# Moving two small expert groups ahead of the token groups of the second and third batch (Trainium2, one core)

## The chip, the cores and the metric

The kernel runs on one core of a Trainium2 chip. The metric is the device time of one execution in microseconds (us). Engines are named as in the profile: PE is TensorE (matrix products), PEld its weight loads, DVE is VectorE, ACT is ScalarE, POOL is GpSimd, SP is SyncE. SP and POOL issue nearly all DMA transfers; each issues in program order, so a transfer that has to wait holds up everything behind it on the same engine ("SPq" is SP as a DMA queue).

## The reference

Two blocks follow each other. The first is an attention over 4 batches of 1088 tokens with 4 heads of 32 columns, whose result is the input x (4352 tokens by 128 columns) of the second, a mixture of 8 experts. All experts see all tokens; P is a table of weights made by 8 rounds of normalizing rows and columns.

```python
# attention: phi(x) = outer product of S1 x and S2 x, 64 features
kv = einsum('bhsf,bhsd->bhfd', phi(k), v);  z = sum(phi(k), axis=2)
x  = einsum('bhsf,bhfd->bhsd', phi(q), kv) / (einsum('bhsf,bhf->bhs', phi(q), z) + 1e-06)
# experts: N, D, E, F = 4352, 128, 8, 1024
P = exp(x @ w_gate - max)
for _ in range(8):
    P /= P.sum(1, keepdims=True) + 1e-09; P /= P.sum(0, keepdims=True) + 1e-09; P *= N / E
out = sum(P[:, e:e+1] * (relu(x @ w1[e]) @ w2[e]) for e in range(E))
```

## The kernel before, in words

**Two phases of expert work.** The program keeps PE busy with expert products while attention and the routing (the 8 rounds that make P) are still running. In this first phase, which ends at 209 us, it works through a list `groups`. A large group `(lo, n, [0])` is expert 0 on 2n tokens from token lo; it needs those columns of xT, the transposed x. A small group `(0, REST, [e])` is expert e on the first 256 tokens only, which are the tokens 0 to 255 of the first batch. Routing weights are put on afterwards, so the groups do not have to wait for P. In the second phase (L1084, L1134) experts 1 to 7 run on all other tokens, with weights first recombined by DVE and POOL ("forms"); that phase takes the remaining 700 us and is not touched.

**Steps.** `steps()` (L886 to L920) is a generator. One step does the first product of one block of the hidden layer (L787, two matmuls of n columns, each as two passes on the chip, so that the profile counts four), a relu on ACT (L789), and the second products of a block that was begun eight steps earlier (`LAG`, L851). A large group has 16 steps, a small one 8, and the whole list 152. Every step is worth a share of `n / 480` (times 16/15 where the seven-product form isn't used). The attention and routing generators yield how many shares of expert work to run between two of their own pieces; `fill` runs steps until that is paid. So the order of PE's instructions is fixed when the program is built, and PE executes it in order.

**Where x comes from.** Batch 0 is made in place on the core (`divide`). Batches 1 to 3 go another way: `tops` (L486) gives numerator and denominator on PE, `over` (L499 to L505, DVE) divides and transposes, and `take_over` writes the result to memory (xd<-xt, L510) and reads it back into xT (xT<-xd, four transfers, L512). For batches 1 and 2 POOL issues both; for batch 3 POOL issues two thirds and SP the rest. A large group that starts at token 1088 needs batch 1, the one at 1920 batches 1 and 2, and so on.

**Where weights come from.** `wb` has six parts of 1024 columns: parts 0 to 2 hold expert 0, parts 3 and 4 first expert 1 (`load_w`) and later another small expert (`small_load`). `prepare_w` issues the loads of expert 1. `bench_load` and `bench_pack` prepare packed weights of experts 4 and 5 for the second phase during attention(2): bench_load(0) brings raw weights into xf0, bench_pack(0) forms their sums on POOL (L201, xf<-xf) and stores them (packed<-xf, L247), and bench_load(2) brings the next raw weights into the same xf0, so SP holds it back until that store has finished. In the routing stage `small_weights` loads experts 3, 5, 6, 7 and one more expert in xf0.

**End of the first phase.** `t0` is the number of steps ahead of the small groups at the list's end. From there on, the program places `first_forms` (DVE, L986 to L990), the weighting of the second item and the forms of five weight halves (`forming`, DVE L1046) among the remaining steps.

Of the kernel before, what the change touches and what calls it, by code (L numbers as in the profile page):

```python
# [53 lines left out]
def kernel(  # L54
# [18 lines left out]
    F = moe_w1.shape[2]  # L73
# [18 lines left out]
    wb = big.tile([P, 6 * F], F32, name="wb")  # L92
# [100 lines left out]
    def load_w(e):  # L193
        w1, w2, ws = (wb[:, F * (3 * e + i):F * (3 * e + i + 1)] for i in range(3))
        w2, ws = w2.rearrange("p (f d) -> p f d", d=DM), ws.rearrange("p (c q d) -> p c q d", c=4, d=H2)
        nc.sync.dma_start(out=w1, in_=moe_w1[e])
        nc.sync.dma_start(out=w2, in_=moe_w2[e].rearrange("(fo fi) d -> fi fo d", fi=P))
        return [w1, w2, None, ws]
# [14 lines left out]
    def sums_of_two(w2, ws):  # L213

        forms(w2[:, 0::2, 0:H2], w2[:, 1::2, 0:H2], w2[:, 0::2, H2:DM], w2[:, 1::2, H2:DM], *(ws[:, i] for i in range(4)),
              False)
        return ws
# [105 lines left out]
    def transpose_k(b, parts=((0, NT),)):  # L323
        kx = loaded["k", b]
        for lo, hi in parts:
            nc.vector.transpose(out=kT[:, 0:NT * P].rearrange("p (t c s) -> p c t s", c=4, s=32)[:, :, lo:hi],
                                in_=kx[:, 0:4 * NT, :].rearrange("p (c t) d -> p c t d", c=4)[:, :, lo:hi])
        nc.vector.transpose(out=kT[:, NT * P:S], in_=kx[:, 4 * NT:SA, :].rearrange("p a d -> p (a d)"))
# [77 lines left out]
    def multiply(c, i):  # L406
        lo, hi = chunks[c]
        nc.vector.tensor_tensor(phs[0][:, i, lo:hi], phs[0][:, i, lo:hi], queries.pop((0, c, i)), op=Alu.mult)
# [192 lines left out]
    def routing():  # L601
# [53 lines left out]
        for b in range(B):  # L655
# [13 lines left out]

    NX = 256  # L670
    REST = 256
    groups = [(0, 256, [0]), (512, 288, [0]), (1088, 416, [0]), (0, REST, [1]), (1920, 416, [0]), (2752, 416, [0]),
              (0, REST, [2]), (3584, 384, [0]), *((0, REST, [e]) for e in (4, 3, 5, 6, 7))]
    SMALL = {g for g, group in enumerate(groups) if group[2][0]}
    DIRECT = {0, *SMALL}
    HELD = 2
# [2 lines left out]
    items = [(g, e) for g, group in enumerate(groups) for e in group[2]]  # L679
# [3 lines left out]
    def direct_of(j):  # L683
        return items[j][0] in DIRECT

    def prepare_w(j):
        e = items[j][1]
        if e not in loaded_w and e < 2:
            loaded_w[e] = load_w(e) if j else first_w
# [101 lines left out]
    def two(k):  # L791

        j, q = blocks[k]
        lo, n, _ = groups[items[j][0]]
        h, ts, (later_h, earlier_h, t13) = hs[k] = room_of(k)

        def step(c):
            f, t = (4 * q + c, 0) if items[j][0] in SMALL else (2 * q + c // 2, c % 2)
            first(k, f, lo + t * n, lo + (t + 1) * n, h[c], k % 2)

        def less(out, a, b):
            nc.vector.tensor_tensor(out, a, b, op=Alu.subtract)

        def sums(c):
            if direct_of(j):
                return
            if c == 4:
                less(t13, later_h, earlier_h)
            elif c == 5:
                less(ts[2], h[3], ts[0])  # L810
                less(ts[3], h[2], ts[2])

        return step, sums
# [63 lines left out]
    def second(k, p):  # L877
        into(items[blocks[k][0]][0], *p)

    def steps():  # L880

        todo, sums_at, t = {}, {}, 0
        for k in range(len(blocks)):
            if k < len(blocks):
                j, q = blocks[k]
                g, e = items[j]  # L886
                n = groups[g][1]
                if q == 0:
                    for i in (j, j + 1):
                        if i < len(items):  # L890
                            prepare_w(i)
                if j == 6 and q == 0:
                    small_load(4, wb[:, 3 * F:4 * F], wb[:, 4 * F:5 * F])
                if q == 1 and j + 1 < len(items) and not direct_of(j + 1):
                    w = loaded_w[items[j + 1][1]]
                    if w[2] is None:
                        w[2] = sums_of_two(w[1], w[3])
                step, sums_ = two(k)
                products = eight if g in DIRECT else seven
            for c in range(4):  # L900
                if k < len(blocks):
                    step(c)
                for do in sums_at.pop(t, ()):
                    do()
                while soon:
                    soon.pop(0)()
                for b, p in todo.pop(t, ()):
                    second(b, p)
                if k < len(blocks) and c == 0:
                    for i in range(2, 10):  # L910
                        sums_at.setdefault(t + i, []).append(lambda i=i, f=sums_: f(i))
                    for i, ps in enumerate(products(k)):
                        if j < len(items) - HELD:
                            todo.setdefault(t + LAG + i, []).extend((k, p) for p in ps)
                        else:
                            held.append((loaded_w[e][1][:, 4 * q + i], hs[k][0][i]))
                share = n / 480 * (16 / 15 if g in DIRECT else 1)
                if later and (c % 2 or share > 0.9 or k >= len(blocks)):
                    later.pop(0)()
                yield share  # L920
                t += 1
# [70 lines left out]
    def small_weights():  # L992

        spare = [pools[0].tile([P, 7, 2, NX], F32, tag="ht", name="ht").rearrange("p s a n -> p (s a n)") for _ in range(2)]
        xf0 = xfs[0].rearrange("p f n -> p (f n)")
        places = {3: (spare[0], 0, 1), 5: (spare[1], 0, 1), 2: (xf0, 0, 1)}
        for e, (t, i, k) in places.items():
            small_load(e, t[:, F * i:F * (i + 1)], t[:, F * k:F * (k + 1)])
        small_load(6, spare[0][:, 2 * F:3 * F], wb[:, 5 * F:6 * F])
        small_load(7, spare[1][:, 2 * F:3 * F], None)  # L1000

    def small_load(e, w1, w2):
        if w1 is not None:
            loaded_w[e] = [w1, None, None, None]
            tc.keep_in_program_order(nc.sync.dma_start(out=w1, in_=moe_w1[e]))
        if w2 is not None:
            w2 = loaded_w[e][1] = w2.rearrange("p (f d) -> p f d", d=DM)
            tc.keep_in_program_order(nc.sync.dma_start(out=w2, in_=moe_w2[e].rearrange("(fo fi) d -> fi fo d", fi=P)))
# [341 lines left out]
    with tc.manual_schedule(engines={engines.DVE, engines.PE}):  # L1350
        for i in range(2):
            multiply(1, i)
        transpose_k(1)
        load_k(2)
        fill(1.25)
        fractions(1, 1)
        fractions(1, 0)
        fill(0.75)
        divide(1)
        keys_ab(1)  # L1360
        fill(0.75)
        query_products(2)
        keys_products(1, 0)
        fill(0.75)
        for i in range(2):
            multiply(2, i)
        keys_products(1, 1)
        fill(1.5)
        fractions(2, 1)
        fractions(2, 0)  # L1370
        keys_products(1, 2)
        fill(0.75)
        divide(2)
        load_v(2)
        load_q(3)
        fill(0.5)
        for b in range(1, B):
            for n in attention(b):
                fill(n)
        for n in routing():  # L1380
            fill(n)
        weights_first()
        t0 = sum(4 * (2 if g in SMALL else 4) for g in range(8))
        assert ran[0] > t0 - 8
        turn_first()
        forming = [lambda e=e, half=half, n=n: form_step(e - 1, half, n) for e, half in AHEAD for n in range(4)]
        for n, (e, half) in enumerate(AHEAD):
            forming.insert(5 * n + 4, lambda e=e, half=half: keep_formed(e - 1, half))
        among = {t0 + 10: [first_forms],
                 t0 + 12: [lambda do=do: do(1) for do in (weights, weighted, turn, xsums)],  # L1390
                 t0 + 18: [lambda: small_load(7, None, wb[:, 4 * F:5 * F])]}
        while ran[0] < 4 * len(blocks):
            for do in among.pop(ran[0], ()):
                do()
            if ran[0] > t0 + 3 and forming:
                forming.pop(0)()
            next(work)
            ran[0] += 1
        assert not soon and not later and not forming and not among
# [40 lines left out]
```

## Time and profile before

| | |
|---|---|
| median of 3 runs | 912.89 us (912.67 to 914.03) |
| the profiled execution's own time | 911.29 us |
| its span, first to last instruction | 909.2 us (2.1 us lie around it) |
| its mean granted TensorE clock | 0.994 |
| PE busy | 892.0 us, 98% of the span |
| DVE, ACT, POOL busy | 734.4, 526.1, 365.5 us |
| HBM read, written | 148.38 MB, 18.65 MB |

The profile page splits the span into 40 slices of 22.7 us and shows each engine's busy share in tenths. Other views are cut from the same execution: the waits (who waited for whom), the chain of work that ended last, the timelines of single engines, and the windows (busy time of each engine in chosen stretches, with the granted clock). Times in the views are in us from the span's start.

### The profile page before, as it was taken

The numbers are of one execution on the slowest core, as the hardware profiler recorded it, in microseconds if no ns is written. First come the engines' busy times: TensorE is split into PE (matmuls) and PEld (weight loads), VectorE is DVE, ScalarE is ACT, GpSimd is POOL, SyncE is SP. The second block draws the span as 40 slices with busy tenths as digits, with TensorE's granted clock in tenths as the row PEclk, the third lists the DMA queues.
The fourth block names the chain that finished last, engine by engine and source line by source line (L and its number), as shares of the span: only waits on it lengthen the run. The fifth ranks groups of instructions, "written<-read, shape, count | busy, mean of one in ns | idle before, by whom it ended". The sixth has DMA issues, their size and how long they took to land.

```text
span 909.2 us, 34647 instructions
## 1 busy us (share of the span) xinstructions
PE 892.0 (98%) x14664; PEld 710.9 (78%) x14664; DVE 734.4 (81%) x1160; ACT 526.1 (58%) x1276; POOL 365.5 (40%) x381
## 2 busy tenths in 40 slices
PE   8969999999999999999999999999999999999997
PEld 6747756688898877787777888999789886788776
DVE  7647778873899888889889897988889788889984
ACT  3325546466655665666566656665755676567652
POOL 3010330040454444545674453435434553544330
PEclk9979999999999999999999999999999999999999
DMA  9896359061577867778787777777676777767740
GB/s 263 261 314 192 118 177 303 1 216 71 169 222 231 240 197 215 219 235 231 214 237 197 222 213 226 214 218 226 200 200 196 234 217 221 227 201 220 198 125 13
DMA packets 150234, 183.97 MB, mean 202 GB/s; under 512 B 16352, under 2 KB 112368, under 8 KB 149696
## 3 DMA queue, kind: packets, MB, share of 16 engines
q1 hardware_dynamic: 143856, 164.17, 61.4%
q0 software_dynamic: 5024, 17.42, 5.4%
q8 instruction: 116, 1.90, 0.8%
q14 instruction: 38, 0.31, 0.1%
q10 hardware_dynamic: 1200, 0.16, 0.1%
HBM read 148.38 MB, written 18.65 MB: 184 GB/s over the span
## 4 chain that ended last, share of the span: by engine, by line
PE 95%; DMA 2%; DVE 1%; issue 0%; SPq 0%; ACT 0%; POOL 0%; ACTq 0%
PE a L1084 37%; PE s L1134 37%; PE a L787 9%; PE s L851 7%; PE a L371 1%; DMA xd<-xt 1%; PE s L866 1%; DMA xT<-xd 1%; PE a L486 1%; DMA qx<-in_q_dram 1%; PE a L1235 0%; PE s L400 0%; PE s L416 0%; PE a L450 0%; PE a L520 0%
## 5 line engine op out<-in xcount | busy, mean ns | idle before, releaser
L1084 PE MATMUL a<-wb,w1f 64*64 64x256 f32 x4144 | 430.0, 377 | 0.0
L1084 PEld LDWEIGHTS a<-wb,w1f 64*64 64x64 f32 x4144 | 269.9, 133 | 37.2 <-issue 2.2
L1084 PE MATMUL a<-xf,w1f 64*64 64x256 f32 x2128 | 229.2, 377 | 0.4 <-issue 0.4
L1098 ACT COPY a<-a 128x256 f32<-128x256 f32 x224 | 80.0, 357 | 212.1 <-PE a L1084 211.9
L1134 PE MATMUL s<-ht,w2r 64*64 64x256 f32 x1344 | 189.2, 376 | 0.0
L1134 PE MATMUL s<-hb,w2r 64*64 64x256 f32 x1344 | 187.5, 376 | 0.0
L201 POOL TENSOR_TENSOR wb<-wb 128x256 f32<-128x256 f32 (+1 forms) x115 | 130.4, 1135 | 125.4 <-DMA wb<-wb 78.6
L1134 PE MATMUL s<-ht,w2f 64*64 64x256 f32 x1216 | 160.3, 376 | 0.0
L1134 PE MATMUL s<-hb,w2f 64*64 64x256 f32 x1216 | 158.4, 376 | 0.0
L1084 PEld LDWEIGHTS a<-xf,w1f 64*64 64x64 f32 x2128 | 139.9, 133 | 19.0 <-issue 1.5
L1134 PEld LDWEIGHTS s<-ht,w2r 64*64 64x64 f32 x1344 | 113.1, 133 | 19.9
L1134 PEld LDWEIGHTS s<-hb,w2r 64*64 64x64 f32 x1344 | 112.3, 133 | 18.3
L789 ACT ACTIVATE hb<-a 128x256 f32<-128x256 f32 (+3 forms) x152 | 66.2, 441 | 82.6 <-PE a L787 74.1
L787 PE MATMUL a<-xT,wb 128*64 128x416 f32 (+3 forms) x448 | 102.6, 462 | 7.6 <-DMA xT<-xd 7.6
L1134 PEld LDWEIGHTS s<-ht,w2f 64*64 64x64 f32 x1216 | 99.0, 133 | 9.1
L1134 PEld LDWEIGHTS s<-hb,w2f 64*64 64x64 f32 x1216 | 98.3, 133 | 8.2
L851 PE MATMUL s<-hb,wb 128*64 128x416 f32 (+3 forms) x408 | 98.9, 455 | 0.0
L201 POOL TENSOR_TENSOR xf<-xf 128x256 f32<-128x256 f32 (+1 forms) x62 | 71.1, 1149 | 61.9 <-DMA xf<-xf 43.2
L1105 DVE TENSOR_TENSOR ht<-a,mid 128x256 f32<-128x256 f32 x112 | 47.2, 422 | 58.6 <-ACT a L1093 40.6
L201 POOL TENSOR_TENSOR wb<-wb,xT 128x512 f32<-128x512 f32 x37 | 51.4, 1388 | 88.3 <-DMA wb<-pT 65.0
L1093 ACT COPY a<-a 128x256 f32<-128x256 f32 x224 | 80.0, 357 | 9.3 <-PE a L1084 1.0
L1096 ACT COPY mid<-a 128x256 f32<-128x256 f32 x224 | 85.0, 379 | 0.0
(203 smaller groups left out, 1636.7 us busy)
## 6 DMA issues: line engine op xcount, KB each, us to landing
w1f<-packed SPq DMA_DIRECT2D x204, 224.0 KB, 5.0
w2r<-in_moe_w_dram SPq DMA_DIRECT2D x56, 512.0 KB, 7.1
w2f<-packed SPq DMA_DIRECT2D x68, 256.0 KB, 4.9
wb<-pT SPq DMA_DIRECT2D x45, 256.0 KB, 4.6
wb<-wb SPq DMA_DIRECT2D x74, 128.0 KB, 4.4
hb<-packed SPq DMA_DIRECT2D x32, 256.0 KB, 6.3
xf<-pT SPq DMA_DIRECT2D x19, 256.0 KB, 4.4
xf<-xf SPq DMA_DIRECT2D x36, 128.0 KB, 4.1
```

The lines of the kernel that those rows point to most:

```text
L201: tc.keep_in_program_order(nc.gpsimd.tensor_tensor(*args, op=op))
L371: nc.tensor.matmul(pv[64 * s:64 * (s + 1), i], kp[0:n, H * t + h].rearrange("p i j -> p (i j)"), vx[0:n, slots[h], t, :], start=(t == 0 an ...
L486: nc.tensor.matmul(pn[64 * s:64 * (s + 1), t, 2 * i:2 * i + 2].rearrange("p h d -> p (h d)"), ph[:, i, s, 64 * t:64 * (t + 1)], kvs[b % 2] ...
L787: nc.tensor.matmul(ph[sl], loaded_w[items[j][1]][0][:, P * f + H2 * s:P * f + H2 * (s + 1)], xT[:, lo:hi], start=True, stop=True, tile_pos ...
L789: nc.scalar.activation(out=out, in_=ph, func=Act.Relu)
L851: nc.tensor.matmul(sums[g][i][H2 * s:H2 * (s + 1)], w, x, start=c == 1, stop=c == per, tile_position=(0, H2 * s))
L1084: nc.tensor.matmul(half_of(r, b, c, n)[rows[s]], w1s[i][rows[r], 1 + form, u, H2 * s:H2 * (s + 1)], xf(i, x)[rows[r]], start=m == opens, s ...
L1093: nc.scalar.copy(b, a)
L1096: nc.scalar.copy(m5s[k, r], c)
L1098: nc.scalar.copy(d, a)
L1105: nc.vector.tensor_tensor(h[:, H3, r], d, m5s[k, r], op=Alu.add)
L1134: nc.tensor.matmul(place[rows[s]], w[form][rows[r], pair, u], h[rows[r], x, pair], start=task in (0, 4) and k in firsts, stop=True, tile_p ...
```

## The change

The list of groups gets another order. In words, with large groups by their first token: before, 0, 512, 1088, e1, 1920, 2752, e2, 3584, then e4, e3, e5, e6, e7; after, 0, 512, e1, 1088, e2, 1920, 2752, e4, 3584, then e3, e5, e6, e7. What goes with it: the load of expert 1 is issued at the third block of the first group instead of when the group ahead of it starts; parts 3 and 4 of wb take expert 2 after expert 1 (`small_load(2)`, placed at the third block of group 1088) instead of expert 4; expert 4 takes the place in xf0 that expert 2 had; the second weights of expert 7 are loaded when the group e4 starts instead of near the end of the phase; and t0 counts nine groups instead of eight, since five small groups at the end have become four.

```diff
-    groups = [(0, 256, [0]), (512, 288, [0]), (1088, 416, [0]), (0, REST, [1]), (1920, 416, [0]), (2752, 416, [0]),
-              (0, REST, [2]), (3584, 384, [0]), *((0, REST, [e]) for e in (4, 3, 5, 6, 7))]
+    groups = [(0, 256, [0]), (512, 288, [0]), (0, REST, [1]), (1088, 416, [0]), (0, REST, [2]), (1920, 416, [0]),
+              (2752, 416, [0]), (0, REST, [4]), (3584, 384, [0]), *((0, REST, [e]) for e in (3, 5, 6, 7))]
...
                 if q == 0:
-                    for i in (j, j + 1):
-                        if i < len(items):
-                            prepare_w(i)
-                if j == 6 and q == 0:
-                    small_load(4, wb[:, 3 * F:4 * F], wb[:, 4 * F:5 * F])
+                    prepare_w(j)
+                if j == 0 and q == 2:
+                    prepare_w(2)
+                if j == 3 and q == 2:
+                    small_load(2, wb[:, 3 * F:4 * F], wb[:, 4 * F:5 * F])
+                if j == 7 and q == 0:
+                    small_load(7, None, wb[:, 4 * F:5 * F])
...
-        places = {3: (spare[0], 0, 1), 5: (spare[1], 0, 1), 2: (xf0, 0, 1)}
+        places = {3: (spare[0], 0, 1), 5: (spare[1], 0, 1), 4: (xf0, 0, 1)}
...
-        t0 = sum(4 * (2 if g in SMALL else 4) for g in range(8))
+        t0 = sum(4 * (2 if g in SMALL else 4) for g in range(9))
...
-                 t0 + 12: [lambda do=do: do(1) for do in (weights, weighted, turn, xsums)],
-                 t0 + 18: [lambda: small_load(7, None, wb[:, 4 * F:5 * F])]}
+                 t0 + 12: [lambda do=do: do(1) for do in (weights, weighted, turn, xsums)]}
```

## The prediction

> **What bounds the kernel now.** First the page: PE is busy for 892.0 of 909.2 us, so only what makes PE wait or run slowly can be won. Its slices show where that is.
>
> ```profile
> PE   8969999999999999999999999999999999999997
> PEclk9979999999999999999999999999999999999999
> ```
>
> The only dip behind the start is in the third slice (45 to 68 us), and the granted clock dips there too. The waits and the chain of work say for what:
>
> ```profile
> PE a L787 <- DMA xT<-xd: 7.6, 1, 7.6
> ```
>
> ```profile
> 46.69 8.46 DMA xd<-xt
> ...
> 57.07 6.22 DMA xT<-xd
> ```
>
> This is the first product of group 1088, which needs batch 1 in xT; x goes out to memory and back, 14.7 us in two transfers. PE's timeline and the windows (wall time, busy time of five engines, granted clock, DMA share, GB/s) give the price:
>
> ```profile
> 55.50 0.41 PE L851 MATMUL s<-hb,wb 128*64 128x288 f32 x1
> 63.53 1.65 PE L787 MATMUL a<-xT,wb 128*64 128x416 f32 x4 [7.63 <-DMA xT<-xd]
> ...
> 65.90 3.90 PE L371 MATMUL a<-v,kp 128*64 128x64 f32 x72
> 69.74 0.92 PE L787 MATMUL a<-xT,wb 128*64 128x416 f32 x4
> ```
>
> ```profile
> 56.00:58.00 2.00, 0.00 (x0) 0.00 (x0) 1.32 (x2) 0.79 (x3) 2.00 (x4) 1.00 1.13 240
> 58.00:60.00 2.00, 0.00 (x0) 0.00 (x0) 1.97 (x4) 0.00 (x0) 1.22 (x3) 0.73 1.09 244
> ...
> 66.00:68.00 2.00, 2.00 (x42) 2.00 (x40) 0.00 (x0) 0.00 (x0) 0.00 (x0) 0.50 0.95 332
> ```
>
> PE stops at 55.9. The clock falls to half at about 58.9 and stays there until about 69.1, so the work from 63.53 to 69.74 (6.2 us) is what takes 3.6 us elsewhere: 0.70 for a first product of 416 columns, 0.48 for second products of 288, 2.39 for keys_sums (L371, at 92.95). **Price of the wait: 7.6 + 2.6 = 10.2 us**, 1.1% of the run.
>
> **The change part by part.** No matmul is added or taken away, so the sum is waits alone.
>
> *The old wait.* Ahead of group 1088 PE now has expert 1: eight first products of 256 columns at 0.43 (3.4 us), the second products of 288 due beside them (six at 0.48, two at 0.24: 3.4), and the pieces of attention(2) that came behind the wait: keys_sums 2.4 and two `tops` at 0.79 (L486 and L490, 37.06 to 37.85). That is 10.8 us: the first product of 1088 comes up at 55.9 + 10.8 = 66.7, while xT landed at 63.3. What hides it is thus 3.4 us more than the transfer needs. `tops` needs times(2,0) and times(2,1), which DVE did at 57.4 and 59.2 and needs to have done by 62 and 65. I take the whole 10.2 us as won.
>
> *Expert 1 loaded earlier.* Its two loads (1 MB, about 3.2 us at the 330 GB/s of the fullest stretches) move on SP from behind the ph loads of batch 3 to before v of batch 2, some 41 us earlier. Between 34 and 42 us the DMA engines are busy 0.79, 0.79, 0.30 and 0.59 in windows of 2 us: 3.1 us are free there, so I cost it at nothing. Without that cover rb of batch 2 and the reading back of batch 1 would come 3.2 us later, at 66.5, still inside the 66.7. At 67 us the queue loses the same load.
>
> *Expert 2 loaded into the place of expert 1.* This is the part that I doubt. In the changed program's order SP issues small_load(2) behind bench_load(2), and bench_load(2) must wait until POOL has packed and stored what bench_load(0) brought, which POOL does after taking batch 2 over. In the run before:
>
> ```profile
> 86.00 0.57 POOL L510 DMA_DIRECT2D xd<-xt  x1 [26.78 <-DVE xt L505]
> 89.38 2.18 POOL L512 DMA_DIRECT2D xT<-xd  x4 [2.80 <-DMA xd<-xt]
> 91.58 4.49 POOL L201 TENSOR_TENSOR xf<-xf 128x256 f32<-128x256 f32 x4
> 96.37 0.58 POOL L247 DMA_DIRECT2D packed<-xf  x1 [0.30 <-POOL xf L201]
> ```
>
> ```profile
> 100.44 2.38 SPq L230 DMA_DIRECT2D xf<-in_moe_w_dram  x4
> ```
>
> Nobody on PE waits for that chain now. After the change expert 2's first product does. Its start: `tops(2,2)` stands behind three steps of 1088 and DVE's `over(2,2)` behind the sums of that group's first four relus. The fourth first product ends at 66.7 + 4 x 0.70 + 3 x 0.43 (second products of expert 1) + 0.79 = 71.6; relu with its start 0.8, the sums (L802, 832 columns) 1.0, over(2,2) with its start 1.7 (84.28 to 86.00 before): POOL issues xd at 75.1. From there by rows: xd until the first xT issue 3.4 (batch 2 before, quiet DMA) to 8.7 (batch 1, 46.69 to 55.43, full DMA). SP issues qa of batch 3 only when ACT has copied it behind four steps of expert 1, at about 62.7, and by batch 2's spacing (39.47 to 47.36) rb at 70.6 or a little sooner; rb, xf and qx took 8.4 us of DMA (75.6 to 84), so until 78 or 79 the DMA is full. That covers over half of xd's way: I take 5.3. Then xT issues 2.2, packing 4.5, 0.3, from the store's issue to bench_load(2) 4.1, its four issues 2.4, and the first weights of expert 2. The 512 KB loads of wb took 5.7 us in full DMA, the 512 KB store packed<-qx 3.6 in quiet: I take 3.6, since little else runs then. Sum 22.4, landing at 97.5.
>
> PE on its side has 16 first products of 416 (11.2), eight second products of 256 (3.4) and 4.9 of 416, three `tops` (2.4), keys_ab (L338, 1.1) and keys_sums (2.4): 25.4 us from 66.7, and wants expert 2 at 92.1. **New wait: 5.4 us.** With xd at 3.4 it is 3.5, with 8.7 it is 8.8. PE being late itself would not change the end, since the weights set it.
>
> *The clock in the new wait.* In the old wait the half clock began 3.0 us after PE's last matmul. A wait of 5.4 us passes that, so I add the same loss of 2.6 us; the bounds are 0 and 4.3 (half clock for a further third of the old wait's 10.2 us, half of that time lost). The Trainium skill ("TensorE: Matmul & The Clock Gate", section "What's actually happening") states that half clock follows an idle window of about 3.4 us and that the windows run freely. By that a 5.4 us wait can straddle two windows, fill neither and keep full clock, which would give 5.4 in the place of 8.0. The trace agrees with its window so far as the 10.2 us at half clock are three times 3.4.
>
> *Logits.* They need batch 3 whole. Before, 9.7 us lie between the end of tops(3,2) (107.9) and the logits (117.6), about what the chain over DVE, SP, xd and xT takes. After the change the work between is five first products of 256 (2.2), second products of 416 (2.8) and five steps of 416 and 256 (5.7), 10.6 us: nothing added.
>
> *Routing and the end of the phase.* The shares put the end of routing at step 114 of 152 before and 116 after. What is left is 38 x 0.86 = 32.8 us before, and four steps of 384 at 1.3 plus 32 x 0.86 = 32.8 after: the same. first_forms stands eight steps (6.9 us) nearer to the second phase; DVE finished it at 192.9 and PE used it at 209.7, so of 16.8 us about 10 remain. The forming spreads over 28 steps in the place of 36, and DVE was idle for 11 us behind it. The other weight loads come early enough in both. Cost nothing; if that cover failed, the second phase would start late by the lack.
>
> **Sum**: -10.2 + 5.4 + 2.6 = -2.2 us against the profiled execution's 911.29, that is 909.1. The median of the runs shown is 1.6 us above that execution, so I predict 912.89 - 2.2 = 910.7.
>
> **The rivals.** A measurement of this kernel can tell about 0.2% from no change, 1.8 us.
>
> *The clock stays full in the new wait.* Then -10.2 + 5.4 = -4.8, 908.1. For it: the wait is 2.4 us longer than the point at which the clock fell, which is not much. Against: the one wait that the trace has did lose it. By the page named above this is a matter of where the window falls.
>
> *No new wait.* Expert 2's weights come in time, or what precedes them takes PE longer: -10.2, 902.7. For it: PE's 25.4 us are a sum without any stall. Against: even with the shortest xd the chain ends 3.5 us late.
>
> *Slower: the new wait costs more than the old one.* The mechanism is the same SP queue. If rb, xf and qx are still draining when xd(2) goes out, xd takes 8.7 as batch 1's did, and expert 2's weights 5.7 in the place of 3.6, for 10.9 + 2.6 = 13.5: +3.3 us, 916.2. It decides for slower once the wait exceeds 7.6 us. For it: batch 1's own rows. Against: at 84 to 86 us before, with that queue drained, the DMA share was 0.05.
>
> *The old wait does not go.* If the earlier load delays batch 1 by more than 3.4 us, PE still waits, and the chain to expert 2 shifts with it: some 2 us more than the forecast, 912.7, about no change. For it: full DMA from 42 to 64 us. Against: the 3.1 free us.
>
> **How the numbers follow.** Chances: forecast 0.46, full clock 0.20, no new wait 0.10, slower 0.16, old wait stays 0.08. The forecast's own range is -10.2 + 3.5 to -10.2 + 8.8 + 2.6, thus 906.2 to 914.1. The range given, 905.6 to 915.2, takes in the longer half clock in part, the full clock with the short wait (906.2, less 0.6 for the spread of the runs) and part of the slower case; it leaves out no new wait and the rest of the slower case, under 2 in 10. Faster by over 1.8 us: over half of the forecast (0.27), nearly all of full clock (0.19) and no new wait (0.10), with a little of the old wait's case, 0.57. Within 1.8 us: 0.23. Slower: 0.20, from the slower case and the forecast's upper end.
>
> **What would show it.** In the changed profile: no wait of L787 for xT<-xd, full clock from 56 to 70 us; a wait of L787 of 3 to 9 us near 92 us for DMA wb<-in_moe_w; SP's bench_load(2) near 91 us and behind it small_load(2); half clock around 95 to 103 us. Full clock there with a wait of 5 us speaks for the first rival. No wait at all near 92 us would make the prediction wrong, as would new waits of PE between 110 and 215 us, in routing or at the second phase's start.

## The result, and the profile after

The changed kernel takes **918.11 us** (median of 20 runs, 914.18 to 921.21) against 912.78 us (20 runs, 910.72 to 915.57) for the kernel before: a ratio of 1.0054, 95% interval 1.0043 to 1.0066. It is slower by some 5 us, where 2.2 us faster was predicted, and above the upper end of the range. The profiled execution took 920.07 us, with a span of 918.1.

The slices of the page show first that the dip in the third slice has gone, and that another has come in the fifth (92 to 115 us):

```profile
PE   8999699999999999999999999999999999999997
PEclk9999899999999999999999999999999999999999
```

The waits of PE in the first phase (engine, line, what it waited for: us in total, times, longest) name what stands there:

```profile
PE a L787 <- DMA wb<-in_moe_w_dram: 8.1, 1, 8.1
PE s L851 <- ACT w L740: 2.1, 1, 2.1
...
PE s L851 <- ACT f L736: 0.6, 1, 0.6
...
PE a L486 <- DVE ph L477: 0.3, 1, 0.3
```

The wait for xT<-xd isn't among them any more. The first line is the wait that the prediction expected, half as long again. The second and third are in no term of the sum: second products that wait for ACT. PE's timeline (start, duration, in brackets the idle time before) places them:

```profile
102.23 1.12 PE L787 MATMUL a<-xT,wb 128*64 128x256 f32 x4 [8.13 <-DMA wb<-in_moe_w_dram]
...
192.32 0.87 PE L787 MATMUL a<-xT,ht 128*64 128x256 f32 x5
195.30 0.65 PE L851 MATMUL s<-hb,ht 128*64 128x256 f32 x4 [2.11 <-ACT w L740]
...
212.77 0.38 PE L1086 MATMUL a<-xf,w1f 64*64 64x256 f32 x2
```

The last line is the first product of the second phase (L1084 in the kernel before, where it stands two lines higher). In the kernel before it was this:

```profile
209.72 0.38 PE L1084 MATMUL a<-xf,w1f 64*64 64x256 f32 x2
```

So the second phase begins 3.05 us later. A second profile of each kernel gave 208.63 and 213.78; by the means of the two, 209.2 and 213.3, it begins 4.1 us later, which lies inside the interval of the ratio (3.9 to 6.0 us). The second phase itself took 701.6 us in the second profile of the changed kernel and 701.8 in that of the kernel before, so the loss lies ahead of it; in the first profile of the changed kernel it took 705.3, which did not come back.

The chain to expert 2's weights, in POOL's timeline and then in SP's:

```profile
75.81 0.57 POOL L510 DMA_DIRECT2D xd<-xt  x1 [10.97 <-DVE xt L505]
84.21 2.18 POOL L512 DMA_DIRECT2D xT<-xd  x4 [7.83 <-DMA xd<-xt]
86.41 4.29 POOL L201 TENSOR_TENSOR xf<-xf 128x256 f32<-128x256 f32 x4
91.00 0.57 POOL L247 DMA_DIRECT2D packed<-xf  x1 [0.30 <-POOL xf L201]
```

```profile
94.85 2.38 SPq L230 DMA_DIRECT2D xf<-in_moe_w_dram  x4
97.29 0.58 SPq L1007 DMA_DIRECT2D wb<-in_moe_w_dram  x1
```

Read from start to start: xd 8.4, the xT issues 2.2, packing 4.3 and 0.3, store to bench_load(2) 3.85, its issues 2.4, and from 97.29 to PE's 102.23 the load itself, 4.9.

The windows (wall time, busy time of PE, PEld, DVE, ACT and POOL, granted clock, DMA share, GB/s) show how full the DMA engines are under xd, and the clock around the wait:

```profile
80.00:82.00 2.00, 2.00 (x15) 1.09 (x13) 1.93 (x5) 0.55 (x2) 0.00 (x0) 1.00 0.86 313
82.00:84.00 2.00, 2.00 (x61) 1.85 (x59) 0.87 (x1) 0.49 (x1) 0.00 (x0) 1.00 0.24 82
...
96.00:98.00 2.00, 0.00 (x0) 0.00 (x0) 1.64 (x3) 0.00 (x0) 0.73 (x1) 1.00 0.64 192
98.00:100.00 2.00, 0.00 (x0) 0.00 (x0) 0.00 (x0) 0.00 (x0) 0.00 (x0) 0.53 0.98 259
...
102.00:104.00 2.00, 1.77 (x8) 1.06 (x10) 0.00 (x0) 0.38 (x1) 1.94 (x4) 0.50 0.90 241
104.00:106.00 2.00, 2.00 (x14) 0.97 (x12) 0.00 (x0) 0.38 (x1) 1.91 (x4) 0.76 0.48 138
```

Half clock holds from 98.14 to 104.97 by the clock records of the trace, so 2.74 us of it fall on work, of which half is lost: 1.4 us.

The wait at 193 us is read on ACT's timeline:

```profile
190.16 0.47 ACT L723 COPY z<-s 64x384 f32<-64x384 f32 x1 [0.26 <-PE s L851]
...
192.41 0.48 ACT L734 COPY w<-s 64x384 f32<-64x384 f32 x1
...
193.39 0.47 ACT L736 COPY f<-s 64x384 f32<-64x384 f32 x1
...
194.77 0.47 ACT L740 COPY w<-s 64x384 f32<-64x384 f32 x1
```

When group 3584 is done, ACT empties its four banks of sums in turn, bank 0 first, with the relus of the steps between. L739 and L740 empty bank 3, the last. A small group keeps its sums in one bank, that of `e % 4` (`into`, `banks = (items[g][1] % 4,)`). Behind group 3584 now stands expert 3, whose bank is 3: its first second product has to wait for the very last copy. Before, expert 4 stood there, whose bank is 0. The wait of 0.6 us at 114 is that of expert 2, in bank 2, behind group 1088. It is not new: in the kernel before, where expert 2 stood behind group 2752, its first second product waited as long, though the view names no releaser:

```profile
158.81 0.65 PE L851 MATMUL s<-hb,xf 128*64 128x256 f32 x4 [0.60 <-issue]
```

ACT's last copy of bank 2 (L736) ended just ahead of it, at 158.71.

### The profile page after: what moved, and what is told of

It is laid out like the page before. It is cut to its first block, busy times and chain, and to the rows that moved or that the text cites. A ratio compares the mean times of both kernels' runs of the same rounds, so it can differ in the third digit from the quotient of the medians.

```text
span 918.1 us, 34646 instructions
## 1 busy us (share of the span) xinstructions
PE 896.4 (98%) x14664; PEld 715.6 (78%) x14664; DVE 739.9 (81%) x1160; ACT 526.5 (57%) x1276; POOL 357.9 (39%) x381
## 4 chain that ended last, share of the span: by engine, by line
PE 91%; DMA 2%; issue 2%; DVE 2%; ACT 1%; POOL 1%; SPq 0%; ACTq 0%; POOLq 0%; DVEq 0%
PE s L1136 37%; PE a L1086 36%; PE a L787 8%; PE s L851 6%; DMA xd<-xt 1%; PE s L866 1%; PE a L371 1%; DMA qx<-in_q_dram 1%; DMA wb<-in_moe_w_dram 1%; PE a L1237 0%; DMA packed<-xf 0%; PE s L400 0%; DVE hb L1118 0%; POOL xf L201 0%; PE a L450 0%
## 5 line engine op out<-in xcount | busy, mean ns | idle before, releaser
L1086 PEld LDWEIGHTS a<-wb,w1f 64*64 64x64 f32 x4144 | 275.8, 133 | 35.7 <-DVE ht L1107 2.5
L1136 PE MATMUL s<-ht,w2r 64*64 64x256 f32 x1344 | 192.2, 377 | 0.0
L1136 PE MATMUL s<-hb,w2r 64*64 64x256 f32 x1344 | 191.1, 377 | 0.0
L201 POOL TENSOR_TENSOR wb<-wb 128x256 f32<-128x256 f32 (+1 forms) x115 | 127.9, 1113 | 113.9 <-DMA wb<-wb 82.5
L1086 PEld LDWEIGHTS a<-xf,w1f 64*64 64x64 f32 x2128 | 142.2, 133 | 18.5 <-issue 1.8
L201 POOL TENSOR_TENSOR xf<-xf 128x256 f32<-128x256 f32 (+1 forms) x62 | 68.4, 1105 | 63.6 <-DMA xf<-xf 47.6
L201 POOL TENSOR_TENSOR wb<-wb,xT 128x512 f32<-128x512 f32 x37 | 49.3, 1334 | 96.4 <-DMA wb<-pT 61.2
L1107 DVE TENSOR_TENSOR hb<-a,mid 128x256 f32<-128x256 f32 x112 | 47.1, 421 | 48.2 <-ACT a L1095 41.7
```

Source lines behind the costliest of these rows:

```text
L201: tc.keep_in_program_order(nc.gpsimd.tensor_tensor(*args, op=op))
L1086: nc.tensor.matmul(half_of(r, b, c, n)[rows[s]], w1s[i][rows[r], 1 + form, u, H2 * s:H2 * (s + 1)], xf(i, x)[rows[r]], start=m == opens, s ...
L1107: nc.vector.tensor_tensor(h[:, H3, r], d, m5s[k, r], op=Alu.add)
L1136: nc.tensor.matmul(place[rows[s]], w[form][rows[r], pair, u], h[rows[r], x, pair], start=task in (0, 4) and k in firsts, stop=True, tile_p ...
```

## The experiments

The theory after this result: the old wait is worth what was predicted; the new wait on expert 2's weights, with its clock, gives the same amount back; the bank of expert 3 (2.1 us) and small waits turn an even exchange into a loss. The rivals: expert 1's earlier load costs something that shows nowhere; or the wait at 193 us would only move elsewhere if it were taken away; or the loss is in the second phase.

**Both kernels once more.** One profile of each.

> The kernel before, unchanged, for a second profile of its second phase, which was 699.5 us long in the first one. If that length is the kernel's own, it is again 699.5; if the executions differ by as much as their times do, between 699 and 703 us.

> The changed kernel, unchanged, for a second profile of its second phase, which was 705.3 us long in the first one. If the change made that phase longer by 5.8 us, it is again near 705; if most of that was this one execution, some 702 us as in the four other kernels run so far.

The second phases, 701.8 and 701.6 us, are alike, so between these two the loss is not in the second phase. The kernel before took 912.3 us, its second phase beginning at 208.63 behind a wait of 7.6 us and half clock from 57.34 to 67.58. The changed one took 917.35; its waits:

```profile
PE a L787 <- DMA wb<-in_moe_w_dram: 8.9, 1, 8.9
PE s L851 <- ACT w L740: 2.1, 1, 2.1
```

Half clock lasted from 96.36 to 106.60, and PE resumed at 102.73, so it costs 1.9 us here. New wait and clock come to 9.5 us in the first profile and 10.8 in this one, on either side of the 10.2 at which the prediction put the old wait; by the clock records that wait came to 10.4 and 9.9 us in the two profiles of the kernel before.

**Only expert 1 moved.** The kernel before with

```diff
-    groups = [(0, 256, [0]), (512, 288, [0]), (1088, 416, [0]), (0, REST, [1]), (1920, 416, [0]), (2752, 416, [0]),
+    groups = [(0, 256, [0]), (512, 288, [0]), (0, REST, [1]), (1088, 416, [0]), (1920, 416, [0]), (2752, 416, [0]),
...
-                    for i in (j, j + 1):
-                        if i < len(items):
-                            prepare_w(i)
+                    prepare_w(j)
+                if j == 0 and q == 2:
+                    prepare_w(2)
```

> The kernel before with one part of the change: expert 1 ahead of group 1088 and its load issued early; experts 2 and 4 stay where they were. The queue theory (the loss sits in expert 2's weights behind bench_load(2) on SP, 8.1 us and 1.4 at half clock, and the gain of the old wait is real) expects that wait gone and no new one: the old wait's 10.2 us are won against before, so about 902.6 us, the second phase starting near 199.5 us instead of 209.7. The rival, that the early load or the earlier end of the first phase costs elsewhere (in the DMA-bound stretch up to 60 us, or in the second phase), expects 907 us or more, with the second phase's length, 699.5 us before, grown by several us.

Measured: 904.69 us, ratio 0.9925 (0.9909 to 0.9941). The clock is full throughout, the second phase begins at 200.93, and no wait for a DMA is left in the first phase. Two small waits are longer or new, both for `mid`, a buffer that DVE fills with transposed keys (L326) and later with transposed logits (L529):

```profile
PE a L338 <- DVE mid L326: 1.8, 1, 1.8
...
PE a L787 <- DVE mid L529: 0.8, 1, 0.8
```

The start is 8.2 us earlier than the mean of the two profiles of the kernel before. The new wait of 0.8 us, at 111 us, takes its part; the other one lies at the kernel's start, 6 to 8 us, and was 1.3 us in one profile of the kernel before and absent in the other. So some 9 of the 10.2 us are accounted for in the profiles, and in the runs 6.8 us were won (5.4 to 8.3 by the interval). Moving expert 1 brings most of what the prediction said, and no wait shows a cost of its earlier load. What makes the change slower is in the rest of it.

**Expert 2's weights ahead of bench_load(2).** The changed kernel with

```diff
                 bench_pack(0)
-                bench_load(2, lambda: halves_in(xfs[0]), 5, 0)
...
             keys_products(b + 1, 2)
             yield 1.4
+            if b == 2:
+                bench_load(2, lambda: halves_in(xfs[0]), 5, 0)
```

which puts it behind small_load(2) on SP's queue.

> The changed kernel with one edit: bench_load(2) is issued at the end of attention(2), behind small_load(2), so that expert 2's weights no longer stand behind it on SP. The queue theory expects the 8.1 us wait near 94 us and the half clock behind it (1.4 us) gone: 918.1 - 9.5 = 908.6 us, the second phase starting near 203.3 instead of 212.8. The rival, that the weights were only the last of several late things there (xT of batch 2 landed near 89 us, xT of batch 3 near 107 us), expects the wait to move to one of these and the time to stay above 913 us.

Measured: 909.05 us, ratio 0.9963 (0.9949 to 0.9976). The wait for wb is gone, and the second phase begins at 204.88. What is left are the two banks:

```profile
PE s L852 <- ACT w L741: 2.1, 1, 2.1
...
PE s L852 <- ACT f L737: 0.4, 1, 0.4
```

So the wait is SP's order and not the size of expert 2's load: the chain xd, packing, store and bench_load(2) was what held it. One thing came unasked. The windows of this run around the bank's wait:

```profile
184.00:186.00 2.00, 0.28 (x4) 0.20 (x6) 0.30 (x1) 1.92 (x5) 1.62 (x2) 1.00 0.46 167
186.00:188.00 2.00, 2.00 (x14) 1.18 (x12) 2.00 (x1) 0.46 (x2) 2.00 (x3) 0.56 0.99 380
188.00:190.00 2.00, 2.00 (x14) 1.16 (x12) 1.97 (x3) 0.39 (x1) 1.21 (x3) 0.59 0.81 222
190.00:192.00 2.00, 2.00 (x22) 1.30 (x19) 2.00 (x3) 0.77 (x2) 1.92 (x2) 1.00 0.03 8
```

A wait of 2.1 us was followed by half clock for 3.41 us (186.23 to 189.64), all of it over work: 1.7 us more.

**Another bank behind group 3584.** The changed kernel with expert 5 (bank 1) there:

```diff
-              (2752, 416, [0]), (0, REST, [4]), (3584, 384, [0]), *((0, REST, [e]) for e in (3, 5, 6, 7))]
+              (2752, 416, [0]), (0, REST, [4]), (3584, 384, [0]), *((0, REST, [e]) for e in (5, 3, 6, 7))]
```

> The changed kernel with one edit: the small groups at the end run in the order 5, 3, 6, 7 instead of 3, 5, 6, 7. A small group of expert e sums in accumulation bank e modulo 4. The bank theory says that expert 3 behind group 3584 waits 2.1 us for bank 3, which ACT empties last of that group's four, and that expert 5 in bank 1 doesn't wait: 918.1 - 2.1 = 916.0 us, and no wait of L851 for ACT near 193 us. The rival, that ACT is simply late there whatever the bank, expects the wait to stay and 918.1 us.

Measured: 915.58 us, ratio 1.0037 (1.0023 to 1.0051), second phase from 211.23. On PE's timeline the second products follow the first ones with no idle time between:

```profile
193.12 0.87 PE L787 MATMUL a<-xT,ht 128*64 128x256 f32 x5
193.76 0.65 PE L851 MATMUL s<-hb,ht 128*64 128x256 f32 x4
```

The start is 1.5 to 2.6 us earlier than in the two profiles of the changed kernel, about the 2.1 us of the wait, and no other wait took its place. The times alone would not show it: the intervals of the two ratios, 1.0037 here and 1.0054 for the changed kernel, overlap. It remains slower than the kernel before: here the wait for wb was 8.0 us and half clock lasted from 97.08 to 107.32 with PE back at 101.57, which makes 8.0 + 2.9 = 10.9 us.

**The same bank in the kernel before.** The order `(4, 3, 5, 6, 7)` at the end becomes `(3, 4, 5, 6, 7)`, and expert 7's second load goes from `t0 + 18` to `t0 + 26`, since expert 4, whose part of wb it takes, comes later.

> The kernel before with experts 3 and 4 changed about at the list's end, so that expert 3 follows group 3584 and sums in bank 3 (the second weights of expert 7, which take the place of expert 4's, are issued eight steps later). The bank theory expects the 2.1 us wait of L851 for ACT that the changed kernel has and this kernel never had, 912.6 + 2.1 = 914.7 us, and up to 1.7 us more if the clock falls in it. The rival, that the wait comes of the changed kernel's lateness, expects 912.6 us.

Measured: 915.59 us, ratio 1.0033 (1.0019 to 1.0047). The waits:

```profile
PE a L787 <- DMA xT<-xd: 7.7, 1, 7.7
PE s L851 <- ACT w L740: 2.1, 1, 2.1
```

The wait appears in a kernel that has none of the rest of the change, as soon as expert 3 follows group 3584. That the bank is its cause is thus shown from both sides.

**Both repairs.** The two edits together, in the changed kernel.

> Both edits, the weights of expert 2 ahead of bench_load(2) and expert 5 ahead of expert 3. If the two losses are separate, they add: 918.1 - 9.5 - 2.1 = 906.5 us. If one hides the other (PE arrives earlier at the bank while ACT does not), some 908.6 us.

Measured: 904.86 us, ratio 0.9918 (0.9905 to 0.9931), with full clock throughout and the second phase from 200.54. That is 4.2 us less than with the weights alone: the 2.1 us of the wait and the 1.7 us that half clock cost behind it there make 3.8. It is also 1.6 us below the expected sum, which took the 9.5 us of the first profile for the new wait and its clock; with the 10.8 of the second it would be 905.2. This is level with the kernel that moves expert 1 alone (904.69): placing expert 2 early wins nothing more that these runs can tell, and group 1920 had no wait in the kernel before that it could have hidden.

**What makes xd slow.** In the changed kernel 8.4 us pass between POOL's issue of xd and that of xT; in the kernel before, 3.4. The candidates are the loads ahead of it on SP's queue: rb, then 512 KB each for xf and qx. First bench_load(1), the 512 KB of qx, was moved behind small_load(2), in the same place as above:

```diff
-            bench_load(1, halves_in_two, 5, 1)
...
+            if b == 2:
+                bench_load(1, halves_in_two, 5, 1)
```

> The changed kernel with bench_load(1), 512 KB for qx, issued at the end of attention(2), behind expert 2's weights, instead of ahead of batch 2's transfer to memory. The queue theory says that xd<-xt of batch 2 took 8.4 us, not the 3.4 of before, because SP's loads still filled the DMA engines: without qx (1.6 us of them at 330 GB/s) it expects some 6.8 us, expert 2's wait shorter by as much, near 6.5 us, and about 916.5 us. The rival, that the length is the transfer's own there, expects 8.4 us and no change.

Measured: 917.5 us, ratio 1.0058 (1.0034 to 1.0081). POOL's timeline:

```profile
75.56 0.57 POOL L510 DMA_DIRECT2D xd<-xt  x1 [10.97 <-DVE xt L505]
83.43 2.18 POOL L512 DMA_DIRECT2D xT<-xd  x4 [7.30 <-DMA xd<-xt]
```

7.9 us: half a microsecond less than in the first profile of the changed kernel where 1.6 were expected, and the wait was 8.3 us. Even that isn't clear of the spread: in the kernel that moves expert 1 alone, where xf and qx both stand ahead, xd took 8.0 us. The expectation failed; qx alone isn't what holds xd. Then all four bench calls of attention(2) went there, which takes the whole 1 MB of xf and qx out of its way:

```diff
-        if b == 2:
-            bench_load(0, lambda: halves_in(xfs[0]), 4, 0)
-            bench_load(1, halves_in_two, 5, 1)
...
-            if b == 2:
-                bench_pack(0)
-                bench_load(2, lambda: halves_in(xfs[0]), 5, 0)
...
+            if b == 2:
+                bench_load(0, lambda: halves_in(xfs[0]), 4, 0)
+                bench_load(1, halves_in_two, 5, 1)
+                bench_pack(0)
+                bench_load(2, lambda: halves_in(xfs[0]), 5, 0)
```

> The changed kernel with the whole preparation for the second phase moved: bench_load(0) and (1), bench_pack(0) and bench_load(2) are issued at the end of attention(2), behind expert 2's weights. Two questions. Why was xd<-xt of batch 2 8.4 us long: if it waits for what SP's queue has in flight, then with xf and qx (1 MB) gone and only rb and 512 KB of expert 2 ahead of it, it takes about 5 us; if the length is its own once it is issued near 76 us, 8 us again. And the wait: the weights of expert 2 now come near 78 us, so none near 94 us, and some 909 us as with the weights put first alone.

Measured: 910.16 us, ratio 0.9947 (0.9919 to 0.9975), second phase from 206.33. POOL's timeline, and the load that now stands on SP's queue where xf and qx stood, 512 KB for expert 2:

```profile
76.34 0.58 POOL L510 DMA_DIRECT2D xd<-xt  x1 [10.98 <-DVE xt L505]
82.44 2.18 POOL L512 DMA_DIRECT2D xT<-xd  x4 [5.52 <-DMA xd<-xt]
```

```profile
72.14 0.69 SPq L1006 DMA_DIRECT2D wb<-in_moe_w_dram  x1
```

6.1 us, about half of the way from 8.4 back to 3.4, and below every xd with xf and qx ahead of it. What SP has in flight is thus a part of xd's time. Its bytes alone don't set it: in this run and in the one before, rb and 512 KB more stand ahead of xd, and it took 6.1 and 7.9 us. Why, and what the other half is, was not separated. The wait for wb is gone, one of 1.0 us for xT ahead of the logits (L520) has come, and the bank's 2.1 us remain, again with a stretch of half clock behind them (187.38 to 190.79).

**The same with the other bank.**

> The same, with expert 5 ahead of expert 3 at the list's end: a candidate for the fastest version. The two edits that paid gave 904.9 us together; with batch 2's transfer less hindered nothing on PE should change further, so about 904.9 us if the critical work is PE's alone by then, and 904 or less if the small waits of PE for DVE and ACT there shrink.

Measured: 904.24 us, ratio 0.9887 (0.9868 to 0.9906). Its ratio is the lowest, touching that of both repairs and just apart from that of expert 1 alone. But these ran at another time, its times (902.42 to 907.49) overlap with theirs (903.88 to 907.06 and 904.45 to 905.47), and its profile, of the slowest of its four executions, isn't the better one: the second phase begins at 203.27, behind waits of 2.5 us for `mid` and 1.6 for xT. Three versions beat the kernel before by 7 to 10 us; which of them is the fastest stays open.

## Why the prediction was wrong

*The old wait, the sum's -10.2: right in mechanism and by the trace.* Group 1088's first product came up at 67.21 us (66.7 predicted), no wait stood ahead of it, and the clock stayed full until the new wait. That the whole of it reaches the time is not shown: moving expert 1 alone won 6.8 us (5.4 to 8.3 by the interval) in the runs and 8.2 in the profiles, with 0.8 us more in a new wait for `mid`.

*The new wait, +5.4: the mechanism was right, the size was off.* It was 8.1 us. The weights landed 4.7 us late: POOL's issue 0.7, xd 3.1, the load of wb 1.3, less 0.4 for packing and the store. PE came 2.0 us late as well (94.1 in the place of 92.1: 0.5 from the start and 1.5 in a sum of 25.4 us that counted no stall). So 4.7 - 2.0 = 2.7 us were missing. The failed step in it is "That covers over half of xd's way: I take 5.3": the DMA was taken as full until 78 or 79 us, and it was at 0.86 in the window from 80 to 82. The measured 8.4 is at the bound of 8.7 that the prediction had from batch 1. The choice of 3.6 for wb "since little else runs then" failed in the same way: the window from 98 to 100 us has a DMA share of 0.98, and bench_load(2)'s 512 KB, issued just ahead, and batch 3's xd, which POOL issued at 96.88, lie in the same stretch.

*The clock, +2.6: 1.4 and 1.9 in two profiles, 2.9 with the other bank.* Inside the bounds given; the wait alone doesn't fix it (below).

*"Routing and the end of the phase ... Cost nothing": this step failed outright.* The prediction's last part had named new waits of PE between 110 and 215 us as what would speak against it, and they came. The step counted shares, loads and forms, all of which held, and left out what the reordering does to the banks of sums. It added 2.1 us; the 0.6 us of expert 2's bank had been there before. The two kernels that change only which bank follows show the 2.1. (Two new waits of 0.3 us at L486, at 35 and 91 us, are in no term of the sum either.) This could be read from the kernel: `e % 4` in `into`, and the order in which ACT empties a group.

The terms as measured in the first profile: -10.2 + 8.1 + 1.4 + 2.1 + 0.6 = +2.0 us, where the start of the second phase moved by 3.05. In the second it is -10.2 + 8.9 + 1.9 + 2.1 + 0.6 = +3.3, and the start moved by 5.15 between the second profiles. So of the 7.5 us between the predicted -2.2 and the measured +5.3, these terms give 4.2 and 5.5. The rest stays open: the waits for `mid` at the kernel's start differ by -0.8 and +1.1 us and go with the execution, and PE's gaps under 0.25 us come to no more than 0.2 us in either first profile.

*The rival "slower: the new wait costs more than the old one"* had the right mechanism and nearly the right lengths, and its point of decision, a wait over 7.6 us, was passed in every profile of the changed kernel. Taken alone it brings the exchange to about nothing in the profiles: 9.5 and 10.8 against 10.2. With the other bank, which leaves this rival by itself, the runs give +2.1 to +4.7 us, of which the waits in that profile account for 1.1 (8.0 + 2.9 and 0.4 for `ph`, less 10.2). How the loss of 5 us divides between this and the bank is therefore known only to a microsecond or two; that both are in it is shown by taking each away.

## What to carry to other kernels

When independent groups of work change places, follow each group's outputs as well as its inputs: who had its accumulators last, and who empties them when. A transfer that is moved to where somebody waits for it takes the price of everything ahead of it on its queue, and where its way falls on loaded DMA engines, the row taken under load is the better estimate: here it was 8.7 us, the measured time 8.4, and the value between 5.3. To move only what stands ahead of the stall (here expert 1) won 6.8 us; the second move had no wait to remove and brought two.

## What the runs showed of the hardware

**Half clock comes in whole stretches of 3.41 us**, and the length of a wait doesn't fix their number. Waits of 7.6 to 8.9 us had two or three of them: 6.83 us behind 8.1 (changed kernel) and behind 7.7 (kernel before with the other bank), 10.24 behind 7.6, 8.0, 8.3 and 8.9. Of six profiles with the 2.1 us wait for the bank, of five kernels, two show one stretch of half clock just after it (expert 2's weights first, and the four bench calls later), and four none. The Trainium skill ("TensorE: Matmul & The Clock Gate", section "What's actually happening") tells of a free-running activity window of 3413 ns and of half clock after an idle one; the stretches agree with that length. But a window need not be wholly idle: in the 3.41 us ahead of 186.23 of the run with expert 2's weights first, PE worked for 1.3 us, 38%, and the clock fell.

What decides between the two outcomes can be read from the clock records. Within a profile, the changes of the clock lie whole multiples of 3.413 us apart: from the first record of full clock to the drop, 92.16 us or 27 of them in the changed kernel, 180.91 us or 53 with expert 2's weights first. They mark a grid of stretches through the whole execution. PE's busy time is the second number here, in the stretch that holds most of the bank's wait, first with expert 2's weights first, then in the kernel before with the other bank:

```profile
182.81:186.23 3.42, 1.30 (x14) 0.62 (x12) 1.46 (x4) 3.16 (x8) 1.85 (x3) 1.00 0.50 177
183.97:187.39 3.42, 1.64 (x14) 0.95 (x10) 1.69 (x4) 3.33 (x10) 0.53 (x1) 1.00 0.71 195
```

The first wait lies whole inside one stretch, and the clock fell at its end; the end of a stretch cuts the second, and the clock stayed full. So it is in all six. Over the first phases of all twelve profiles, half clock followed each stretch at full clock with 1.34 us of work or less, and none with 1.64 or more; no run moves the grid on purpose. By these figures a wait of 5.4 us, as predicted, would lose the clock wherever it fell, since at least 2.7 us of it lie in one stretch. The prediction's rival with full clock, which took a window to be wholly idle, does not hold here.

**Other banks are not enough.** The Trainium skill ("Perfetto Trace Analysis", section "Matmuls") has independent groups rotate through different PSUM banks, so that emptying one overlaps the next group's matmuls. The groups here do use different banks, and the rule holds only by which bank comes first: behind a group of four banks, expert 3 in the bank emptied last waited 2.11 us, and expert 5 in the second one not at all.

**A store on POOL's queue beside a full queue of SP's.** The same xd of batch 2 (576 KB, from its issue to that of xT) took 3.4 us with DMA idle ahead of it. With rb, xf and qx issued ahead of it on SP's queue it took 8.0 to 8.9 in six profiles, without qx 7.9, and with 512 KB for expert 2 in the place of xf and qx 6.1 and 6.6.
